# An RWKV block with a soft MoE behind it: three banks of g per block through DMA planes, the decayed state on ScalarE, a new order list

## The chip, the cores and the metric

The kernel runs on one core of one Trainium2 chip. The metric is the device time of one launch in microseconds. The engines are named as in the profile: PE (TensorE), with its weight loads shown apart as PEld, DVE (VectorE), ACT (ScalarE), POOL (GpSimd) and SP (SyncE, which here only issues DMAs). All inputs and outputs are float32.

## The reference

Three layers follow one another. The shapes: 4 batches, 8 heads, 768 steps, 48 values per head, so 3072 tokens of 384 values; 2048 hidden values; 8 experts of 4 slots each.

```python
# attention: a state per batch and head, decayed by w at each step
for t in range(S):
    cur = einsum('bhd,bhe->bhde', u * k[t], v[t])
    y[t] = einsum('bhd,bhde->bhe', r[t], state + cur)
    state = w[t][..., None] * state + einsum('bhd,bhe->bhde', k[t], v[t])
# hidden layer on x = y as [3072, 384]
h = x @ w_in;  g = h * cos(h);  x = g @ w_out
# soft mixture of experts
logits = x @ phi                        # [3072, 32]
d = softmax over tokens;  c = softmax over slots
slots = d.T @ x;  per expert: relu(slots @ w1) @ w2;  out = c @ slots_out
```

The kernel never forms `g @ w_out` for all tokens. It multiplies phi into w_out first, so that the logits come from g by a product with a 2048x32 matrix (`p_sb`), and it sums `d.T @ g` over the tokens (`E`) before w_out is applied.

## The kernel before

**Blocks and banks.** The 3072 tokens are 24 blocks j of 128 (6 per batch). Attention works on one block in two chunks c of 64 tokens: with scans over the decays (`scan`, `sp`), transposes of w, r and k, and matmuls A, U and y. The state goes from chunk to chunk: `e_z` (line 258) multiplies `st_state` by the decay over a chunk and gives z, 128x192; `e_rz` (267) has ACT copy z into the operand of y; `e_st` (271) adds the chunk's U to z and gives the next `st_state`. At the first chunk of a batch z is zeroed instead, so 44 of the 48 are products, all on DVE.

The hidden layer of a block t is four banks q of 128 tokens x 512 hidden values. `b_h` (423) makes one bank in PSUM with nine matmuls; `turns` (ACT), `rest` (DVE), `cos` (ACT) and `mul` (DVE) turn it into g, and the PSUM bank is free after `mul`. Two PSUM buffers hold h, up to bank number `ATT`; from there on h takes a buffer of attention's pool.

**Two ways to turn a bank.** The logits need g with hidden values on the partitions. In the first way four PE transposes (`gT`, `b_t`, line 466) write a PSUM bank and ACT (some of the last banks DVE) copies it out (`gc`, 474). In the second, through planes, `gz` (481) splits the 32-bit words of g into two planes of 16-bit halves, on ACT for every third bank and on GpSimd for the others (`GSPLIT`), `gd` (488) stores both planes in DRAM and `gx` (492) brings them back with a transposing DMA. Both DMAs are issued from SP's queue. Then four small matmuls (`l`, 496) add the bank to the logits. Banks 12 to 75, blocks 3 to 18, go through planes; the others use PE. There are four buffers for split planes and four for transposed banks. Banks that PE transposes use one PSUM buffer before bank `ATT`, and the pool of h from there on.

**Order.** `HEAD` (917) is a list of step names. The steps are issued in this order, and each engine, SP's queue too, runs its own instructions in the order of the list; an instruction waits at the head of its engine until what it needs is there. SP's queue carries the loads of w, r, k and v (`lw`, `lr`, `lk`, `lv`: one DMA per block each; `lz`: four), the planes' DMAs, and the expert weights.

**The end.** After every two blocks the logits go through an online softmax (`sum` to `es`), in which `E` adds `d.T @ g`. At `att` attention's memory is given up and SP is handed the first six of 16 expert weights, of 1536 KB each; each load waits until the tiles that lay in its place are free. Four more replace the parts of w_in, and the rest follow. The code behind the list (752 to 913) makes slots, experts (`hidden`, `expert_out`) and outputs.

Of the kernel before, what the change touches and what calls it, by code (L numbers as in the profile page):

```python
# [921 lines left out]
d2a.i.4 ksn.1 lv.1 d2a.i.5 wf.2 raw.i.6 lk.2 d2b.i.4 lz.1 lr.2 abs.i.5 A.1 y.0 mask.1 q.o.0 xh.0 whi.4 lw.3 xm.0 d2b.i.5 xc.0 wn.4.1 rz.1.0 wc.4.1
d2a.o.0 U.1 lz.2 scan.2 st.1.0 abs.o.0 d2b.o.0 raw.o.1 sr.2 wn.4.0 whi.5 z.1.1 q.i.7 q.i.6 lr.3 h.0.0 abs.i.7 oT.0 d2a.i.7 ru.2 lv.2 wc.4.0 oc.0
st.1.1 wn.5.0 kT.2 turns.0.0 wc.5.0 rz.1.1 d2a.i.6 sp.2 wn.5.1 wc.5.1 abs.i.6 wT.3 z.2.0 wf.3 ks.2 kN.2 rest.0.0 raw.o.2 lw.4 d2b.i.7 ksn.2 y.1 oT.1
d2b.i.6 scan.3 xh.1 rT.2 oc.1 xm.1 cos.0.0 whi.6 xc.1 abs.o.1 h.0.1 lk.4 mul.0.0 L.2 q.o.1 gT.0.0 U.2 bo.2 st.2.0 wn.6.1 sr.3 whi.7 d2a.o.1 wc.6.1
# [8 lines left out]
mul.1.2 rz.4.1 oT.15 h.2.0 gc.1.1 z.6.0 d2a.o.6 oc.15 kT.5 oc.14 sp.5 lw.8 wf.6 d2b.o.6 close gT.1.0 lw.7 ks.5 l.0.2 turns.2.0 bo.5 rT.5 gc.1.0 lr.7
oT.13 oc.13 z.5.0 oT.12 ru.6 rest.2.0 cos.2.0 gT.1.2 l.1.0 l.1.1 y.4 oc.12 L.5 xh.4 bs.5 gc.1.2 D.5 om.3 rT.6 xm.4 kN.5 turns.2.1 mul.2.0 scan.6 sr.6
xc.4 pc.3 bo.6 gT.1.3 lk.7 h.2.2 sp.6 pT.3 ksn.5 gc.1.3 rest.2.1 gT.2.0 bs.6 L.6 l.1.2 ps.3 l.1.3 l.0.3 U.5 turns.2.2 rest.2.2 A.5 cos.2.1 sum.0
rz.6.0 rz.5.0 lc.0 gc.2.0 lv.7 mul.2.1 st.5.0 h.2.3 mask.5 max.0 cos.2.2 kT.6 lz.6 mul.2.2 exp.0 z.5.1 wT.7 gT.2.1 h.3.0 turns.2.3 xt.0 ks.6 rest.2.3
# [4 lines left out]
mask.7 kT.8 gz.3.1 lk.9 rz.7.0 U.7 mul.4.1 bo.8 gz.4.1 gx.3.2 gd.3.1 turns.4.0 rest.4.0 gx.3.3 st.7.0 gx.3.0 bs.8 gx.3.1 h.4.2 wT.9 cos.4.0 D.8 l.2.1
lr.10 es.0 l.3.0 turns.4.2 l.2.2 l.2.3 wf.9 lk.10 mul.4.0 l.3.1 gz.4.0 z.7.1 ks.8 l.3.2 rest.4.2 l.3.3 gd.4.0 sum.1 A.8 lc.1 cos.4.2 scan.9 st.7.1
mask.8 kN.8 rz.7.1 max.1 h.5.0 mul.4.2 kT.9 ksn.8 exp.1 gx.4.0 xt.1 turns.5.0 sr.9 z.8.0 U.8 rest.5.0 cos.5.0 h.4.3 ks.9 ru.10 xr.1 st.8.0 xd.1 lw.11
gz.4.2 mul.5.0 wT.10 turns.4.3 dT.1 kN.9 rz.8.0 z.8.1 rest.4.3 st.8.1 dc.1 cos.4.3 lr.9 lz.8 ltok.1 gz.5.0 bo.10 sp.9 h.5.1 E.1.0 ksn.9 mul.4.3 lv.9
# [4 lines left out]
sp.11 bo.12 l.5.1 gx.5.2 turns.6.3 st.10.0 gx.5.3 D.10 A.10 rest.6.3 z.10.1 lv.11 l.4.3 rest.6.0 cos.6.3 z.12.0 l.5.2 st.10.1 cos.6.0 mul.6.3 rz.10.1  # L950
kT.11 ru.11 l.5.3 gz.6.3 sum.2 lz.9 gz.6.1 mul.6.0 ks.11 lz.10 es.1 h.6.2 gz.6.0 lc.2 mask.10 max.2 turns.6.2 gd.6.0 rest.6.2 kN.11 wT.12 bo.11 exp.2
xt.2 cos.6.2 rT.11 h.7.1 z.11.0 xr.2 mul.6.2 wf.12 xd.2 turns.7.1 rest.7.1 cos.7.1 gz.6.2 lr.13 y.9 dT.2 dc.2 L.11 lw.13 ltok.2 ksn.11 h.7.0 U.11
scan.12 E.2.0 lk.13 st.11.0 rz.11.0 y.10 mul.7.1 xh.9 turns.7.0 cmb.0.0 h.7.3 bs.11 gd.6.3 rest.7.0 xh.10 D.11 z.11.1 xl.9 gz.7.1 gd.6.1 lz.11 sr.12
# [104 lines left out]
```

## Time and profile before

| | us |
|---|---|
| three timed runs | 502.78, 502.20, 499.11 |
| their median | 502.2 |
| the profiled execution | 500.44 |
| its span, from the first to the last instruction | 498.7 |

| engine | busy us | share of the span | instructions |
|---|---|---|---|
| PE | 453.5 | 91% | 6261 |
| PEld | 340.1 | 68% | 6261 |
| DVE | 421.5 | 85% | 819 |
| ACT | 322.2 | 65% | 684 |
| POOL | 145.2 | 29% | 169 |

The mean granted clock of PE over the span is 0.993 of full speed. The chain that ended last, followed back from the last instruction, lies on PE for 56% of the span, on DVE for 14%, on DMA for 11%, on ACT for 6%, on SP's queue for 4% and on POOL for 2%; 5% is time in which the engine waited for nothing that is shown.

Busy time of PE is a union: matmuls overlap in the pipe, a single one lasts longer than the distance to the next, and the drain of the pipe before a wait counts as busy. In a group of instructions the first number after the bar is the sum of their durations, the second the mean of one; what follows the second bar is the idle time of the engine just before them, and what ended it.

### The profile page before, as it was taken

Reading aid. Unit: us, or ns where it says so; the run is one execution under the profiler, and the core shown is the slowest. Engines: PE = TensorE matmul, PEld = TensorE weight load, DVE = VectorE, ACT = ScalarE, POOL = GpSimd, SP = SyncE. Lnnn points to the kernel's source line nnn. Section 1 sums busy time; section 2 is a strip of 40 time slices with the busy share of each in tenths; the row PEclk is TensorE's granted clock in tenths of the full one; section 3 lists DMA queues with packets and bytes.
Section 4 is the critical chain, followed back from the end, with each engine's and each line's share of the span. In section 5 each row is a group of like instructions: output and inputs, shape, how many; then the busy total and the mean of one; then the engine's idle time right before and its main releaser. Section 6 shows DMA issues by size and latency. Waiting matters only on the chain.

```text
span 498.7 us, 15329 instructions
## 1 busy us (share of the span) xinstructions
PE 453.5 (91%) x6261; PEld 340.1 (68%) x6261; DVE 421.5 (85%) x819; ACT 322.2 (65%) x684; POOL 145.2 (29%) x169
## 2 busy tenths in 40 slices
PE   1678999999999899997999998998999999998993
PEld 1456788887777577765867666676777787865573
DVE  3999999999989999997999998997999976765242
ACT  5699998877575576664565864675656764664242
POOL 2422233323323705423334344223612100002110
PEclk9999999999999999998999999999999999999998
DMA  9999978346989969999498899988995579789938
GB/s 229 298 278 219 178 209 147 66 77 138 153 142 203 194 144 202 216 148 225 113 191 209 152 216 198 192 188 166 147 215 132 113 282 411 283 343 356 348 104 278
DMA packets 221188, 101.01 MB, mean 203 GB/s; under 512 B 195776, under 2 KB 201152, under 8 KB 221120
## 3 DMA queue, kind: packets, MB, share of 16 engines
q1 hardware_dynamic: 221120, 100.05, 86.7%
q8 instruction: 49, 0.80, 0.7%
q14 instruction: 19, 0.16, 0.1%
HBM read 61.75 MB, written 21.50 MB: 167 GB/s over the span
## 4 chain that ended last, share of the span: by engine, by line
PE 56%; DVE 14%; DMA 11%; ACT 6%; issue 5%; SPq 4%; POOL 2%; ACTq 0%; POOLq 0%; DVEq 0%
PE h L437 9%; PE h L439 8%; PE h L438 8%; DMA gx<-gs 7%; PE l L503 3%; PE E L599 3%; PE gT L471 3%; DMA rn<-in_r_dram 2%; PE y L283 2%; PE hps L790 2%; PE so L827 2%; PE A L204 2%; DVE pt L166 2%; PE U L255 2%; DVE g L456 2%
## 5 line engine op out<-in xcount | busy, mean ns | idle before, releaser
L437 PE MATMUL h<-wu,x 128*128 128x512 f32 (+1 forms) x288 | 122.3, 425 | 1.6 <-DVE g L464 1.6
L439 PE MATMUL h<-wu,x 128*128 128x512 f32 (+1 forms) x288 | 113.6, 395 | 0.0
L438 PE MATMUL h<-wu,x 128*128 128x512 f32 (+1 forms) x288 | 113.1, 393 | 0.0
L460 ACT ACTIVATE g<-g,half_pi 128x512 f32<-128x512 f32 (+1 forms) x97 | 69.4, 719 | 37.8 <-DVE g L456 37.0
L452 ACT ACTIVATE g<-h 128x512 int32<-128x512 f32 (+1 forms) x96 | 57.0, 596 | 53.3 <-PE h L439 43.2
L485 POOL COPY zg<-g 128x1024 uint16<-128x1024 uint16 x42 | 46.6, 1112 | 117.3 <-DVE g L464 72.1
L456 DVE SCALAR_TENSOR_TENSOR g<-g,h 128x512 f32<-128x512 int32 (+1 forms) x96 | 64.8, 677 | 11.3 <-ACT g L452 10.5
L464 DVE TENSOR_TENSOR g<-g,h 128x512 f32<-128x512 f32 (+1 forms) x96 | 64.3, 675 | 4.6 <-ACT g L460 3.9
L437 PEld LDWEIGHTS h<-wu,x 128*128 128x128 f32 x288 | 54.5, 189 | 17.3 <-DVE g L464 3.4
L439 PEld LDWEIGHTS h<-wu,x 128*128 128x128 f32 x288 | 54.3, 189 | 12.4
L438 PEld LDWEIGHTS h<-wu,x 128*128 128x128 f32 x288 | 54.5, 189 | 8.7
L218 POOL TENSOR_SCALAR_AFFINE_SELECT lt<-bo 64x512 f32<-64x512 f32 x48 | 35.5, 740 | 82.8 <-ACT bo L246 68.0
L171 POOL TENSOR_TENSOR ru<-rn,u_b 128x384 f32<-128x384 f32 x24 | 26.2, 1091 | 49.7 <-DMA rn<-in_r_dram 27.1
L230 DVE COPY_PREDICATED lt<-cs,A 64x256 f32<-64x256 uint32 x72 | 32.3, 448 | 2.8 <-PE A L204 1.4
L269 ACT COPY rzs<-z 64x192 f32<-64x192 f32 x96 | 33.3, 347 | 2.0 <-PE y L283 1.2
L187 DVE TENSOR_TENSOR lt<-rT,pt 64x512 f32<-64x512 f32 x48 | 32.8, 683 | 1.0 <-PE rT L143 0.4
L166 DVE TENSOR_TENSOR_SCAN pt<-wf,ini_f 128x520 f32<-128x520 f32 x24 | 32.8, 1367 | 0.1
L158 DVE TENSOR_TENSOR_SCAN qt<-wf,one_b 128x520 f32<-128x520 f32 x24 | 30.1, 1253 | 0.6 <-ACT wf L153 0.5
L503 PE MATMUL l<-gx,p_sb 128*32 128x128 f32 x512 | 23.4, 280 | 7.6 <-DMA gx<-gs 7.4
L172 POOL TENSOR_TENSOR ru<-ru,kn 128x384 f32<-128x384 f32 x24 | 27.9, 1163 | 4.5 <-DMA kn<-in_k_dram 2.7
L283 PEld LDWEIGHTS y<-lt,rzs 128*32 128x32 f32 x1536 | 23.9, 110 | 6.6 <-issue 5.3
L599 PE MATMUL E<-g,dt 128*32 128x512 f32 (+1 forms) x208 | 25.2, 567 | 2.4 <-ACT dt L580 1.6
(175 smaller groups left out, 807.3 us busy)
## 6 DMA issues: line engine op xcount, KB each, us to landing
we<-in_moe_w_dram SPq DMA_DIRECT2D x16, 1536.0 KB, 9.1
gs<-zg SPq DMA_DIRECT2D x64, 256.0 KB, 3.3
rawo<-in_moe_w_out_dram SPq DMA_DIRECT2D x8, 768.0 KB, 4.5
wn<-in_w_dram SPq DMA_DIRECT2D x24, 192.0 KB, 4.5
rn<-in_r_dram SPq DMA_DIRECT2D x24, 192.0 KB, 4.5
kn<-in_k_dram SPq DMA_DIRECT2D x24, 192.0 KB, 4.6
vn<-in_v_dram SPq DMA_DIRECT2D x24, 192.0 KB, 4.0
rzs<-in_v_dram SPq DMA_DIRECT2D x96, 48.0 KB, 3.0
```

Of the source, the lines that this page charges most:

```text
L166: nc.vector.tensor_tensor_scan(pt, wf[:, 0:NS * SEG], ini_f, 0.0, ALU.mult, ALU.add)
L218: nc.gpsimd.affine_select(out=lt[j % 2][h, a], in_=bo_t[j][h, a].unsqueeze(2).to_broadcast([64, NS, C]), pattern=[[0, NS], [-1, C]], compa ...
L437: nc.tensor.matmul(half[:, f], lhsT=xh[:, c, :], rhs=wh, start=(c == 0), stop=False)
L438: nc.tensor.matmul(half[:, f], lhsT=xl[:, c, :], rhs=wh, start=False, stop=False)
L439: nc.tensor.matmul(half[:, f], lhsT=xh[:, c, :], rhs=wl, start=False, stop=(c == KD - 1))
L452: nc.scalar.activation(gt.bitcast(I32), hp, AF.Copy, bias=0.25, scale=1.0 / TWO_PI)
L456: nc.vector.scalar_tensor_tensor(out=gt, in0=gt.bitcast(I32), scalar=-TWO_PI, in1=hp, op0=ALU.mult, op1=ALU.add)
L460: nc.scalar.activation(gt, gt, AF.Sin, bias=half_pi[:, 0:1])
L464: nc.vector.tensor_tensor(out=gt, in0=gt, in1=hp, op=ALU.mult)
L485: copy(zg, g_t[t, q].bitcast(U16).rearrange("p (f i) -> p i f", i=2))
L503: nc.tensor.matmul(lps_t[g][32 * m:32 * m + 32, o:o + TB], lhsT=p_sb[:, 4 * q + m, :], rhs=gt[:, m * 128:(m + 1) * 128], start=first, stop ...
L599: nc.tensor.matmul(ps[32 * q:32 * q + 32, cols], lhsT=dt_[:, tt, :], rhs=g_t[2 * g + tt, q][:, cols], start=(tt == 0), stop=(tt == 1))
```

## The change

- Banks with q = 3 no longer go through planes, but banks 0 to 2 of block 19 do: 51 banks (blocks 3 to 19, three each) instead of 64. The sixteen banks q = 3 of blocks 3 to 18 are transposed by PE, the three of block 19 no longer.
- All planes are split by GpSimd (`GSPLIT = "p"`).
- From block `JZ` = 5 on, z is made by ACT, as four activations with a scale per partition, one for each pair of heads. `JZP` = 24 lies beyond the last block, so GpSimd makes none.
- `ATT` goes from 77 to 81: four more banks of h stay in the pool of two buffers.
- `GMUL` could put `mul` on GpSimd; its list of q is empty, so no bank is.
- The order list is a new one from its first entries on. After `y.23`, the last step on PE that attention has, 13 banks of h follow in the list before and 8 in the new one; after `att`, 6 in both. In the new list, the step that comes next on ACT after the z of block 5 and later is a `cos` or `turns` in 23 of 35 cases.

```diff
@@ -43,10 +43,12 @@
     NTW = 6
     NLATE = 3
     JA = 6
+    JZ, JZP = 5, 24
     NSPLIT = 4
-    ATT = 77
-    GX = range(12, 76)
-    GSPLIT = "app"
+    ATT = 81
+    NGS = 51
+    GMUL = (12, 80, [])
+    GSPLIT = "p"
     NZG = 4
     NGX = 4
     ORDERED = {mybir.EngineType.PE, mybir.EngineType.DVE, mybir.EngineType.Activation, mybir.EngineType.Pool, mybir.EngineType.SP}
@@ -67,7 +69,7 @@
     ps_l = ps_stack.enter_context(tc.tile_pool(name="ps_l", bufs=1, space=PSUM))
     ps_m = ps_stack.enter_context(tc.tile_pool(name="ps_m", bufs=1, space=PSUM))
     ps_a = ps_stack.enter_context(tc.tile_pool(name="ps_a", bufs=3, space=PSUM))
-    gs_p = ctx.enter_context(tc.tile_pool(name="gs", bufs=len(GX), space=bass.MemoryType.DRAM))
+    gs_p = ctx.enter_context(tc.tile_pool(name="gs", bufs=NGS, space=bass.MemoryType.DRAM))
     a_stack = ctx.enter_context(ExitStack())
     nat = a_stack.enter_context(tc.tile_pool(name="nat", bufs=1))
     aw = a_stack.enter_context(tc.tile_pool(name="aw", bufs=2))
@@ -261,7 +263,11 @@
             nc.vector.memset(z, 0.0)
         else:
             pc = segs(q_t[j][0], 1, 1).rearrange("p (s c) j -> p s c j", c=2)
-            nc.vector.tensor_tensor(out=z, in0=st_state, in1=pc[:, :, c, :].to_broadcast([128, HP, D]), op=ALU.mult)
+            if j < JZ:
+                (nc.vector if j < JZP else nc.gpsimd).tensor_tensor(out=z, in0=st_state, in1=pc[:, :, c, :].to_broadcast([128, HP, D]), op=ALU.mult)
+            else:
+                for p in range(HP):
+                    nc.scalar.activation(z[:, p], st_state[:, p], AF.Copy, scale=pc[:, p, c])
         z_t[j, c] = z
 
     def e_rz(j, c):
@@ -461,7 +467,8 @@
 
     def b_mul(t, q, hf=None):
         gt, hp = bank(t, q, hf)
-        nc.vector.tensor_tensor(out=gt, in0=gt, in1=hp, op=ALU.mult)
+        pool = GMUL[0] <= NBK * t + q < GMUL[1] and q in GMUL[2]
+        (nc.gpsimd if pool else nc.vector).tensor_tensor(out=gt, in0=gt, in1=hp, op=ALU.mult)
 
     def b_t(t, q):
         gt = g_t[t, q]
@@ -915,99 +922,98 @@
 
 
 HEAD = """
...
-cs neg raw.i.1 q.i.1 raw.i.0 abs.i.1 d2a.i.1 q.i.0 lw.0 lw.1 wT.0 lr.0 abs.i.0 raw.i.3 d2b.i.1 lk.0 misc d2a.i.0 whi.1 d2b.i.0 wT.1 wf.0 scan.0 sr.0
...
-gx.8.1 mul.9.1 ksn.13 lw.15 rest.9.0 gd.8.2 sp.13 bs.13 h.9.3 cos.9.0 lw.16 xh.11 mul.9.0 rT.13 D.13 turns.9.3 gz.9.1 z.13.0 h.9.2 wf.14 xl.11
...
-gT.20.0 rest.20.3 turns.20.1 xl.22 gx.18.2 cos.20.3 y.23 cmb.2.2 l.18.2 l.19.1 l.19.2 l.19.3 mul.20.3 rest.20.1 l.18.3 cmb.2.3 xh.23 gT.20.3 cos.20.1
...
+raw.i.1 q.i.1 raw.i.0 d2a.i.1 abs.i.1 cs lw.0 q.i.0 z.0.0 lw.1 abs.i.0 lk.0 d2b.i.1 lr.0 d2a.i.0 d2b.i.0 wT.0 rz.0.0 misc wf.0 whi.0 neg wT.1 raw.i.3
...
+mul.9.2 wf.14 es.3 h.10.1 turns.10.0 rest.10.0 z.13.0 gz.9.2 ru.14 cos.10.0 gx.9.0 gT.9.3 gx.8.1 L.13 turns.10.1 mul.10.0 l.9.0 bs.13 rest.10.1 l.8.0
...
+cos.21.2 mul.21.2 gT.21.2 h.21.1 xh.22 es.9 gc.20.2 turns.21.0 xl.22 y.23 rest.21.0 l.20.2 cos.21.0 l.20.3 turns.21.1 mul.21.0 gc.21.2 gT.21.0 gc.21.0
...
```

## Rows read from the trace of the kernel before

**Rows 1.** Windows (stretch, length, busy us and count per engine, clock, DMA, GB/s)

```profile
95.00:395.00 300.00, 283.95 (x4073) 212.39 (x4067) 279.45 (x560) 192.99 (x419) 111.40 (x115) 0.99 0.89 169
395.00:453.00 58.00, 55.45 (x585) 41.62 (x586) 41.63 (x99) 35.16 (x78) 0.00 (x0) 1.00 0.86 318
```

**Rows 2.** Waits of PE, 95:345 (for whom: total us, times, longest)

```profile
PE l L503 <- DMA gx<-gs: 7.4, 8, 2.9
PE h L437 <- DVE g L464: 1.6, 3, 1.0
PE kT L143 <- DVE st_state L272: 1.3, 1, 1.3
...
PE A L204 <- DVE st_state L272: 0.8, 1, 0.8
```

**Rows 3.** Waits of PEld, 95 to 345 us

```profile
PEld l L503 <- DMA gx<-gs: 11.5, 13, 3.2
```

**Rows 4.** Timeline of PE, 229:240 (start, us, what, idle before it)

```profile
230.92 0.42 PE L503 MATMUL l<-gx,p_sb 128*32 128x128 f32 x8 [2.93 <-DMA gx<-gs]
```

**Rows 5.** Windows of the stretch behind that wait

```profile
231.00:235.00 4.00, 4.00 (x20) 2.99 (x21) 1.16 (x3) 0.21 (x1) 1.04 (x1) 0.65 1.04 276
```

**Rows 6.** Timeline of SP's queue, 222 to 232 us

```profile
223.34 1.51 SPq L490 DMA_DIRECT2D gs<-zg  x3
224.91 5.61 SPq L494 DMA_TRANSPOSE gx<-gs  x3
```

**Rows 7.** Issues of SP by line: ns min/median/max

```profile
L494 SPq DMA_TRANSPOSE gx<-gs x64: 1226/1292/3645, 124.3 to 395.5; - x64
...
L490 SPq DMA_DIRECT2D gs<-zg x64: 332/524/2352, 120.0 to 393.5; - x64
```

**Rows 8.** Chain of waits, 440 to 480 us (start, us, what)

```profile
443.28 0.44 PE gT L471 x4
...
473.81 5.36 PE so L827 x96
```

**Rows 9.** Groups by line, whole run (busy us, mean ns, idle before)

```profile
L485 POOL COPY zg<-g 128x1024 uint16<-128x1024 uint16 x42 | 46.6, 1112 | 117.3 <-DVE g L464 72.1 <-issue 40.5 <-ACT g L452 4.1
...
L269 ACT COPY rzs<-z 64x192 f32<-64x192 f32 x96 | 33.3, 347 | 2.0 <-PE y L283 1.2
...
L485 ACT COPY zg<-g 128x1024 uint16<-128x1024 uint16 x22 | 23.0, 1044 | 1.3 <-DMA gx<-gs 0.8
...
L477 ACT COPY gt<-gT 128x512 f32<-128x512 f32 x25 | 14.5, 585 | 5.1 <-PE gT L471 3.2 <-PE l L503 1.9
...
L246 ACT COPY bo<-bo 64x4 f32<-64x4 f32 x48 | 9.3, 193 | 1.8 <-DVE bo L241 0.7
...
L550 ACT ACTIVATE z<-dl,nb 128x65 f32<-128x65 f32 (+1 forms) x11 | 3.9, 351 | 0.5 <-DVE nb L529 0.2
```

**Rows 10.** Groups by line, DVE, 95 to 395 us

```profile
L264 DVE TENSOR_TENSOR z<-st_state,qt 128x192 f32<-128x192 f32 x34 | 16.5, 484 | 0.1
```

**Rows 11.** The decayed state's line over the run: ns min/median/max

```profile
L264 DVE TENSOR_TENSOR z<-st_state,qt x44: 296/351/1461, 21.9 to 390.5; 128x192 f32<-128x192 f32 x44
```

**Rows 12.** Timeline of all engines, 218 to 220 us

```profile
218.90 1.03 POOL L485 COPY zg<-g 128x1024 uint16<-128x1024 uint16 x1
218.99 1.16 DVE L264 TENSOR_TENSOR z<-st_state,qt 128x192 f32<-128x192 f32 x1
```

**Rows 13.** Windows of the end of the run

```profile
400.00:430.00 30.00, 30.00 (x307) 23.21 (x306) 21.19 (x50) 17.04 (x36) 0.00 (x0) 1.00 0.93 363
430.00:440.00 10.00, 9.89 (x58) 7.45 (x57) 7.33 (x20) 6.81 (x18) 0.00 (x0) 1.00 0.60 190
440.00:472.00 32.00, 29.08 (x432) 18.78 (x434) 15.60 (x41) 14.40 (x36) 4.76 (x6) 1.00 0.99 382
```

**Rows 14.** Timeline of PE, 402 to 404 us

```profile
402.51 1.10 PE L283 MATMUL y<-lt,rzs 128*32 128x64 f32 x64
```

**Rows 15.** The page's slices: GB/s in 40 slices

```profile
GB/s 229 298 278 219 178 209 147 66 77 138 153 142 203 194 144 202 216 148 225 113 191 209 152 216 198 192 188 166 147 215 132 113 282 411 283 343 356 348 104 278
```

More of the change, by code (lines that the diff above doesn't have):

```diff
@@ L922 @@
[L922 to L925, printed above, removed]
@@ L934 @@
[L934 to L937, printed above, removed]
@@ L942 @@
[L942 to L945, printed above, removed]
@@ L950 @@
[L950 to L953, printed above, removed]
@@ new lines @@
+oT.14 gc.1.1 d2b.o.6 close rz.4.1 xc.3 sp.5 turns.2.0 lz.5 oT.15 oc.14 oc.15 gT.1.0 l.0.2 wf.6 rest.2.0 rT.5 ru.5 oT.12 gc.1.0 oc.12 oT.13 oc.13
+gT.1.2 cos.2.0 bo.5 l.1.0 ru.6 z.5.0 y.4 gc.1.2 om.3 scan.6 L.5 mul.2.0 bs.5 pc.3 turns.2.1 lw.7 xh.4 l.1.1 kT.5 gT.1.3 D.5 sr.6 pT.3 ps.3 h.2.2 xm.4
+ks.5 rest.2.1 bo.6 cos.2.1 sp.6 kN.5 mul.2.1 gc.1.3 bs.6 rT.6 gT.2.0 turns.2.2 z.6.0 L.6 l.1.2 rest.2.2 l.1.3 l.0.3 ksn.5 sum.0 xc.4 lk.7 A.5 rz.5.0
+U.5 lc.0 mask.5 lv.6 cos.2.2 h.2.3 max.0 kT.6 exp.0 gc.2.0 D.6 mul.2.2 turns.2.3 lr.7 xt.0 st.5.0 ru.7 z.5.1 xr.0 h.3.0 wT.7 rest.2.3 ks.6 xd.0 gT.2.1
@@ new lines @@
+turns.6.0 ksn.10 sum.2 mul.6.3 U.10 lc.2 rest.6.0 scan.11 max.2 lv.11 gz.6.1 h.6.2 cos.6.0 mul.6.0 gT.6.3 D.10 exp.2 lz.9 xt.2 xr.2 ru.12 turns.6.2
+lz.10 rest.6.2 st.10.0 lr.11 cos.6.2 sr.11 xd.2 h.7.1 dT.2 A.10 mul.6.2 dc.2 ltok.2 turns.7.1 mask.10 h.7.0 z.10.1 kT.11 rz.9.1 st.10.1 gz.6.0
+rest.7.1 gz.6.2 cos.7.1 sp.11 z.11.0 mul.7.1 E.2.0 turns.7.0 E.2.1 gd.6.0 y.9 rT.11 gd.6.1 gc.6.3 ks.11 bo.12 rest.7.0 rz.10.1 ru.11 cos.7.0 gd.6.2
+h.7.3 L.11 gx.6.0 wT.12 mul.7.0 xh.9 gz.7.0 turns.7.3 kN.11 bo.11 rest.7.3 ksn.11 xl.9 cos.7.3 h.7.2 cmb.0.0 lv.12 mul.7.3 lw.13 wf.12 turns.7.2 bs.11
@@ new lines @@
+scan.14 gd.9.2 cos.10.1 U.13 st.13.0 sr.14 D.13 mul.10.1 h.10.2 A.13 gx.8.2 rz.13.0 bo.14 gz.10.0 gx.9.1 h.10.3 mask.13 wT.15 gc.9.3 kT.14 l.8.1
+gx.9.2 l.9.1 turns.10.2 z.13.1 rz.12.1 l.8.2 lr.15 l.9.2 sp.14 l.8.3 turns.10.3 st.13.1 rest.10.2 l.9.3 cos.10.2 y.12 rest.10.3 sum.4 lz.13 ks.14 lc.4
+lv.14 cos.10.3 ru.15 mul.10.2 rT.14 wf.15 gd.10.0 mul.10.3 max.4 xh.12 L.14 h.11.1 kN.14 rz.13.1 exp.4 xt.4 xr.4 h.11.0 gz.10.2 turns.11.1 xd.4
+gz.10.1 rest.11.1 ksn.14 z.14.0 cos.11.1 gx.10.0 xl.12 dT.4 lw.17 U.14 y.13 dc.4 ltok.4 mul.11.1 E.4.0 gd.10.2 st.14.0 rz.14.0 xh.13 h.11.3 scan.15
@@ new lines @@
+gx.11.0 z.15.1 st.15.1 rz.15.0 l.10.3 es.4 turns.12.1 l.11.0 rest.12.1 bo.17 wf.17 gx.11.1 A.15 h.12.3 scan.17 gx.11.2 l.11.1 rz.15.1 cos.12.1
+mul.12.1 mask.15 l.11.2 xh.14 gz.12.0 l.11.3 lw.19 z.16.0 turns.12.3 kT.16 xl.14 sum.5 ru.16 lc.5 gz.12.1 rest.12.3 h.13.0 max.5 exp.5 ks.16 xt.5
+lw.18 cos.12.3 gz.12.2 turns.13.0 wT.18 lz.15 sr.17 xr.5 mul.12.3 rT.16 kN.16 gd.12.0 xd.5 bo.16 ksn.16 dT.5 rest.13.0 lz.16 bs.16 dc.5 gd.12.2 h.13.1
+ltok.5 L.16 cos.13.0 E.5.0 mul.13.0 U.16 rz.16.0 lr.18 cmb.1.0 turns.13.1 lv.17 st.16.0 rest.13.1 h.13.2 D.16 z.16.1 gd.12.1 cos.13.1 sp.17 wf.18
@@ new lines @@
+gx.13.2 gx.13.0 cos.14.3 cmb.1.3 wf.19 mul.14.3 h.14.2 gd.14.0 gc.13.3 rT.18 scan.19 l.13.0 l.13.1 turns.14.2 xh.16 bs.18 l.13.2 gz.14.1 l.13.3
+rest.14.2 l.12.3 gT.14.3 lz.17 cos.14.2 sum.6 L.18 h.15.1 lc.6 mul.14.2 xl.16 max.6 kT.18 lv.19 turns.15.1 A.17 exp.6 rest.15.1 xt.6 ks.18 h.15.0
+gd.14.1 lr.20 xr.6 D.18 cos.15.1 z.18.0 gx.14.0 xd.6 kN.18 mask.17 dT.6 ksn.18 l.14.0 U.18 ltok.6 mul.15.1 lw.21 gx.14.1 st.18.0 dc.6 lk.20 ru.19
+sr.19 gz.14.2 rz.18.0 l.14.1 E.6.0 turns.15.0 wT.20 sp.19 h.15.2 rest.15.0 gz.15.1 kT.19 bo.19 z.18.1 st.18.1 gd.14.2 wf.20 E.6.1 cos.15.0 turns.15.2
@@ new lines @@
+mul.15.0 gz.15.0 rest.15.2 lz.18 A.18 gd.15.1 ks.19 gx.14.2 cos.15.2 mul.15.2 lk.21 h.15.3 mask.18 kN.19 bs.19 gc.14.3 rz.17.1 turns.15.3 ksn.19
+rest.15.3 h.16.1 cos.15.3 turns.16.1 lw.22 rT.19 y.17 scan.20 gz.15.2 mul.15.3 rest.16.1 z.19.0 D.19 xh.17 gd.15.0 gd.15.2 h.16.0 rz.18.1 gx.15.1
+cos.16.1 ru.20 L.19 xl.17 gx.15.0 mul.16.1 turns.16.0 rest.16.0 gx.15.2 gT.15.3 U.19 sr.20 st.19.0 cos.16.0 gc.15.3 h.16.3 sp.20 rz.19.0 z.19.1
+turns.16.3 es.6 wT.21 l.15.0 mul.16.0 lz.19 l.14.2 st.19.1 l.15.1 l.15.2 l.15.3 l.14.3 gz.16.0 gd.16.0 lw.23 rest.16.3 wf.21 scan.21 A.19 sum.7 kT.20
@@ new lines @@
+gc.22.3 cos.23.3.0 rest.23.3.1 cmb.2.5 E.10.0 mul.23.3.0 h.22.2 turns.23.0 rest.23.0 gT.22.0 cos.23.2 mul.23.2 cos.23.3.1 cos.23.0 turns.22.2
+mul.23.3.1 we.9 mul.23.0 gc.22.0 h.23.1 rest.22.2 gT.23.0 cos.22.2 turns.23.1 mul.22.2 l.22.0 l.22.1 gT.22.2 rest.23.1 gc.23.0 gT.23.2 l.23.0 gc.22.2
+cos.23.1 l.22.2 mul.23.1 l.22.3 gT.23.1 we.6 gc.23.2 gT.23.3 gc.23.3 we.7 gc.23.1 l.23.1 tab l.23.2 l.23.3 sum.11 lc.11 E.10.1 quart.11 max.11 exp.11
+late0 dT.11 ltok.11 dc.11 E.11.1 E.11.0 es.10 we.8 cmb.2.6 esl.11.1 esl.11.0 cmb.0.6
```

135 lines of the change are left out of this document (61 added, 74 removed).

## Prediction

> **What bounds the kernel now.** I first read busy time by stretch [rows 1]. From 95 to 395 us, where attention blocks and hidden banks run together, PE is busy 283.95 of 300 us and DVE 279.45; ACT has 107 us to spare, GpSimd 189. From 395 to 453 us PE is busy 55.45 of 58 and nothing competes with it. So what is to be won lies in the first stretch: 16 us in which PE has nothing to do. PE is the bound on average, but DVE at 93% is so close that every wait on it is likely to be felt.
>
> Next the waits of PE in that stretch [rows 2]. The largest is not DVE's: the logits matmuls stand 7.4 us, 8 times, for a plane that its transposing DMA has not delivered. Then come waits for DVE; the three largest, 1.6 for a product g, 1.3 and 0.8 for a new state, make 3.7. The weight loads wait longer for planes, 11.5 us [rows 3]: the 4.1 us between the two figures is time in which the matmul pipe drains and still counts as busy. One plane wait is 2.93 us long [rows 4], and behind it the granted clock is 0.65 on average over 4 us [rows 5], so part of that stretch went at the lower level, 1.2 of 2.4 GHz: at 0.65 about 35% of the 4 us, 1.4 us, was lost on top.
>
> Why the plane was late is seen on SP's queue [rows 6]: three stores of planes and three transposes fill it from 223.3 to 230.5, back to back. One transpose takes SP 1.29 us, one store 0.52, by their medians [rows 7]. SP is a third resource near its limit here.
>
> **The change, part by part.** *Planes.* Sixteen banks (the fourth of blocks 3 to 18) leave the planes, three (0 to 2 of block 19) enter; 64 planes become 51. On PE each bank that leaves costs four transposes, 0.44 us in the chain [rows 8]: +7.0 us before 395, -1.3 after, **+5.7 us**. PE is the bound there, so I charge it in full. SP loses 13 x (1.29 + 0.52) = 23.5 us of issuing, and the DMA engines 13 stores and 13 transposes. The plane waits with their clock loss are 7.4 + 1.4 = 8.8 us; between none and all of it goes. A fifth fewer planes on a queue that is full should take more than its share, and the loads of r, k and v behind them come sooner too: I take two thirds, **-6**. Of the drained 4.1, and as much again behind waits on DVE, **-3** (0 to -5).
>
> *The copies into planes.* ACT loses 22 x 1.044 = 23.0 us, GpSimd gets 9 more of 1.11, 10 us [rows 9]. GpSimd has the room; what waits is the plane behind it, and SP behind that, since each store is in SP's order: 0, with up to +3 if GpSimd's queue stands behind a load of r. Transposed banks are copied out of PSUM: sixteen more on ACT and two fewer, and DVE loses the one of bank 77: 14 x 0.585 = +8.2 us on ACT [rows 9]. All 45 such copies share one PSUM buffer up to bank 80; in the list a block's transposes come about once per block, so the buffer is free: 0, at most +1. The same bound holds for the four banks whose h stays longer in the two-buffer pool.
>
> *The decayed state.* Of 44 products, 35 leave DVE (38 from block 5 on, less the three that are zeroed). In the stretch one costs 484 ns [rows 10], 351 at the median and up to 1461 [rows 11]: the long ones stand beside a GpSimd copy, as at 218.99, where the product took 1.16 us while the copy that began at 218.90 ran [rows 12]. So 35 x 0.484 = 16.9 us of DVE go, stalls included; by the median 12.3. The Trainium skill (GPSIMD Engine Reference, Key points) says the same of instructions with two SBUF inputs, and its Perfetto Trace Analysis (Optimizing Scalar/DVE Operations) warns that moving work between GpSimd and VectorE might not help; the scans still have two SBUF inputs and meet nine more copies, which by that rule would leave the median's 12.3 rather than 16.9.
>
> DVE's idle time in the stretch rises from 20.5 to 37.4 us. Waits on an engine shrink roughly as its spare time grows: 20.5/37.4 = 0.55, so of the 3.7 us **-1.7** go (0 to -3.7).
>
> On ACT each product becomes four instructions of 128x48 with a scale per partition. The nearest rows are a 64x4 copy, 193 ns, a 64x192 copy, 348, and a 128x65 activation with an operand per partition, 351 [rows 9]. Between the copies 48 columns would be 229 ns; I take 290, halfway to 351, as the operand is there but the function is simpler: 1.16 us a product, 40.6 in all. The Trainium skill (ScalarE: Activation LUTs, Rules for kernel authors) says to multiply on VectorE rather than ScalarE, and budgets about 0.3 us plus 0.83 ns an element; an estimate by it is 1.36 us a product, 47.6 in all. Net, ACT gains 26 us on 107 spare, so the sum gets 0. It is not free of risk: ACT waits in order, and a product stands at the head of its queue until DVE has added the state before it; in the list 23 of the 35 have a turns or cos next behind them on ACT, and PE waits for those through DVE and the two h buffers. Cover gone, this is the second rival.
>
> *The list.* The order is new from its first entries on. The part that I can price is the end: after the last y, 13 hidden banks followed, now 8. From 402.51 [rows 14] to the last bank's transposes at 443.28 [rows 8] one bank takes 3.1 us, so attention ends some 15 us later against the end. SP sends the first six expert weights as attention's tiles come free, so they come later, and DMA has to make it up: against 411 GB/s, the highest slice of the page [rows 15], the time from 400 to 472 leaves 48 x 30 + 221 x 10 + 29 x 32 = 4.6 MB unused [rows 13], 11 us. 15 - 11 leaves 4 us, less than the last weights have in hand if they have landed by 472 and serve the end of the matmuls that run to 479 [rows 8]. I take 0 (up to +7). The first 95 us and the end hold the same work; 0 (-2 to +2).
>
> Sum: 5.7 - 6 - 3 - 1.7 = **-5.0 us**. The profiled execution took 500.4 us, its span 498.7; the three timed runs have the median 502.2. With the profiled one the middle of the four is 501.3, and I set the sum against that: **496.3 us**; that is 495.4 from the profiled execution and 497.2 from the median.
>
> **Rivals.** *DVE was the bound.* If PE's idle time was the shadow of a full DVE and SP, all of it goes. Then the stretch is PE's busy time, 284 + 7 = 291 us, 9 less, and 1.3 go after it: 490 us. For it: DVE at 93%, and attention is now spread over five more banks. Against: a third of PE's named waits are of other kinds.
>
> *ScalarE becomes the wait.* If one in three of the 23 x 1.16 us reaches PE, that is +8.9 (10.4 by the page's price), and with +5.7 and half of the relief, -5.5, the time is 501.3 + 9.1 = 510 us. It decides once ACT's queue has less than 1.16 us in hand before a turns. For it: the state's chain goes from DVE to ACT and back twice per block. Against: in the stretch ACT is busy 193 us, and would be some 220 of 300.
>
> *The waits move.* The relief is real but the order list sets who waits: planes come in time, something else is late, and PE has 5.7 us more work: 501 to 507, I say 504. For it: the rest of PE's waits are scattered over many lines.
>
> *Weights come late.* The forecast plus 6: 502 us.
>
> *It does not do what it says* only in two harmless parts: the list of banks whose product goes to GpSimd is empty, and the limit for GpSimd's decayed state is never reached.
>
> **How the numbers follow.** Forecast 0.40 (its own range 492 to 501), DVE 0.20, waits move 0.18, ScalarE 0.13, weights 0.09. The range of 8 in 10 is **486 to 507**: DVE's case with 4 us of room for a new list below, the waits that move above; most of ScalarE's case is left out. A per cent, which is about what this kernel's runs can tell, is 5 us: under 497.2 lie DVE's case and over half of the forecast, 0.45; over 507.2 most of ScalarE's and the edge of the moved waits, 0.18; between, 0.37.
>
> **What would show it.** From block 5 on, DVE's decayed state gone and its busy share in the stretch below 90%; four short ACT instructions per product of 0.23 to 0.35 us; plane waits of PE under 3 us in all and no stretch at a low clock behind one; PE busy 5 to 6 us more. Wrong would be: PE waiting for turns or the new state more than 5 us, or for expert weights.

## The result: 485.0 us after, 500.7 before, and the profile after

The changed kernel took **485.02 us** (median of four runs, 484.38 to 485.73); the kernel before, run on the same chip, 500.65 (four runs, 497.31 to 502.78). The ratio is 0.969, with the interval 0.963 to 0.976. The forecast was 496.3 with the range 486 to 507: the sign was right, the forecast gain was a third of what came, and the measured time lies just below the range. The profiled execution took 484.42 us with a span of 482.6, which is 16.1 us less than before.

Windows of the kernel after (stretch, length, busy us and count of PE, PEld, DVE, ACT, POOL, granted clock, DMA share, GB/s):

```profile
0.00:95.00 95.00, 79.86 (x1092) 61.65 (x1093) 84.07 (x122) 82.05 (x161) 27.03 (x45) 1.00 0.87 209
95.00:395.00 300.00, 296.61 (x4192) 229.55 (x4194) 277.89 (x560) 218.83 (x566) 117.06 (x123) 1.00 0.82 159
395.00:482.60 87.60, 75.41 (x1038) 54.60 (x1027) 42.78 (x103) 38.96 (x91) 6.68 (x10) 0.98 0.84 306
```

The first and last of these stretches in the kernel before, which [rows 1] does not have:

```profile
0.00:95.00 95.00, 76.74 (x1003) 59.51 (x1007) 84.47 (x123) 79.61 (x154) 27.09 (x45) 1.00 0.91 209
395.00:498.70 103.70, 92.83 (x1199) 68.18 (x1196) 57.56 (x138) 49.56 (x114) 6.69 (x10) 0.98 0.81 292
```

These rows and [rows 1] account for all 16.1 us. PE's idle time falls from 18.3 to 15.1 us in the first 95 us (-3.1), from 16.05 to 3.39 from 95 to 395 (-12.7), and rises from 10.9 to 12.2 behind that (+1.3). PE's busy time is 1.6 less (453.5 to 451.9), although it has 52 more transposes. DVE is as busy from 95 to 395 us as before, 277.89 against 279.45: the state's products are gone, but more banks fit into the same 300 us.

Waits of PE after, 95 to 345 us (for whom: total us, times, longest), to be read against [rows 2]:

```profile
PE dT L580 <- ACT ksn L236: 0.9, 1, 0.9
PE E L606 <- ACT dt L587: 0.7, 1, 0.7
PE E L606 <- DVE ltok L593: 0.7, 1, 0.7
PE U L257 <- DVE lt L232: 0.3, 1, 0.3
```

No wait for a plane is left, and none for a product g or a new state. The page's chain after (section 4) says the same in one line; before, PE had 56% of it, DMA 11% and SP's queue 4%:

```profile
PE 75%; DVE 11%; ACT 9%; issue 2%; DMA 2%; SPq 0%; ACTq 0%; DVEq 0%
```

Groups by line after (busy us, mean ns, idle before), for the moved work; they answer to [rows 9] and [rows 10]:

```profile
L478 PE MATMUL gT<-cs,g 128*128 128x128 f32 x180 | 26.9, 276 | 0.1
L510 PE MATMUL l<-gx,p_sb 128*32 128x128 f32 x408 | 16.5, 277 | 0.0
L492 POOL COPY zg<-g 128x1024 uint16<-128x1024 uint16 x51 | 56.2, 1109 | 107.7 <-DVE g L471 74.6 <-issue 19.3 <-PE h L445 6.5
L270 ACT ACTIVATE z<-st_state,qt 128x48 f32<-128x48 f32 x140 | 35.2, 324 | 2.9 <-DVE st_state L278 2.5
```

The number behind the bar is a union of the instructions' times, not their sum, as the section on the profile before has it: 140 x 324 ns would be 45.4 us. So the 140 activations are 35 products at 35.2/35 = 1.01 us. Four in a row on the timeline of ACT after (start, us, what):

```profile
218.41 1.00 ACT L270 ACTIVATE z<-st_state,qt 128x48 f32<-128x48 f32 x4
```

And the chain of the kernel after at its end (start, us, what), beside [rows 8]:

```profile
425.95 0.44 PE gT L478 x4
...
457.46 5.36 PE so L834 x96
```

From these transposes to these matmuls it is 31.51 us; before it was 473.81 - 443.28 = 30.53. So the end gives back 1.0 us of what was won ahead of it.

### The profile page after: what moved, and what is told of

Its sections match the earlier page's. It is cut to its first block, busy times and chain, and to the rows that moved or that the text cites. A ratio compares the mean times of both kernels' runs of the same rounds, so it can differ in the third digit from the quotient of the medians.

```text
span 482.6 us, 15486 instructions
## 1 busy us (share of the span) xinstructions
PE 451.9 (94%) x6313; PEld 345.8 (72%) x6313; DVE 404.7 (84%) x783; ACT 339.8 (70%) x816; POOL 150.8 (31%) x178
## 4 chain that ended last, share of the span: by engine, by line
PE 75%; DVE 11%; ACT 9%; issue 2%; DMA 2%; SPq 0%; ACTq 0%; DVEq 0%
PE h L443 13%; PE h L445 12%; PE h L444 12%; PE E L606 4%; PE y L289 4%; PE gT L478 4%; PE l L510 4%; PE A L206 3%; PE hps L797 2%; PE so L834 2%; PE wT L145 2%; PE U L257 2%; PE rT L145 2%; PE kT L145 2%; PE kN L213 2%
## 5 line engine op out<-in xcount | busy, mean ns | idle before, releaser
L492 POOL COPY zg<-g 128x1024 uint16<-128x1024 uint16 x51 | 56.2, 1109 | 107.7 <-DVE g L471 74.6
L466 ACT ACTIVATE g<-g,half_pi 128x512 f32<-128x512 f32 x97 | 69.4, 718 | 23.4 <-DVE g L462 22.5
L458 ACT ACTIVATE g<-h 128x512 int32<-128x512 f32 x96 | 57.2, 596 | 40.5 <-PE h L445 32.3
L462 DVE SCALAR_TENSOR_TENSOR g<-g,h 128x512 f32<-128x512 int32 x96 | 64.9, 677 | 8.0 <-ACT g L458 6.6
L471 DVE TENSOR_TENSOR g<-g,h 128x512 f32<-128x512 f32 x96 | 64.6, 676 | 7.8 <-ACT g L466 6.6
L443 PEld LDWEIGHTS h<-wu,x 128*128 128x128 f32 x288 | 54.2, 188 | 15.8 <-DVE g L471 2.5
L173 POOL TENSOR_TENSOR ru<-rn,u_b 128x384 f32<-128x384 f32 x24 | 25.5, 1061 | 44.3 <-DVE bo L243 12.9
L270 ACT ACTIVATE z<-st_state,qt 128x48 f32<-128x48 f32 x140 | 35.2, 324 | 2.9 <-DVE st_state L278 2.5
L232 DVE COPY_PREDICATED lt<-cs,A 64x256 f32<-64x256 uint32 x72 | 32.2, 447 | 2.0 <-PE A L206 0.5
L160 DVE TENSOR_TENSOR_SCAN qt<-wf,one_b 128x520 f32<-128x520 f32 x24 | 31.3, 1305 | 1.1 <-ACT wf L155 1.1
L168 DVE TENSOR_TENSOR_SCAN pt<-wf,ini_f 128x520 f32<-128x520 f32 x24 | 30.2, 1257 | 0.1
L174 POOL TENSOR_TENSOR ru<-ru,kn 128x384 f32<-128x384 f32 x24 | 25.7, 1071 | 9.2 <-DMA kn<-in_k_dram 7.6
```

The costliest lines, as they stand in the source:

```text
L270: nc.scalar.activation(z[:, p], st_state[:, p], AF.Copy, scale=pc[:, p, c])
L443: nc.tensor.matmul(half[:, f], lhsT=xh[:, c, :], rhs=wh, start=(c == 0), stop=False)
L458: nc.scalar.activation(gt.bitcast(I32), hp, AF.Copy, bias=0.25, scale=1.0 / TWO_PI)
L462: nc.vector.scalar_tensor_tensor(out=gt, in0=gt.bitcast(I32), scalar=-TWO_PI, in1=hp, op0=ALU.mult, op1=ALU.add)
L466: nc.scalar.activation(gt, gt, AF.Sin, bias=half_pi[:, 0:1])
L471: (nc.gpsimd if pool else nc.vector).tensor_tensor(out=gt, in0=gt, in1=hp, op=ALU.mult)
```

## The experiments

"Old list" and "new list" are the order lists of the two kernels. "The parts" are the other edits: the fourth bank on PE, all planes from GpSimd, the decayed state (z) on ScalarE. Each kernel was timed beside the kernel before on the same chip; ratios are to that one. Differences between two experiments are of their medians. Most pairs come from different chips, on which the kernel before had medians of 500.65 to 502.76, so a difference of 2 us or less says little. `ATT` = 81 and the planes of block 19 go with the new list in all that follows; no run separates them from it.

### Parts without the list, list without the parts

The theory at this point was that the list and the parts work only together; the rival, that one of the two carries the gain alone. The old list with the parts replaces `gz`, `gd`, `gx` of each fourth bank by `gT` and `gc` in the places of `gd` and `gx` and keeps 48 planes. The new list without the parts puts `gz`, `gd` and `gx` of these banks at 18, 43 and 75% of the way from their `mul` to their `l`; these places were chosen, so the size of what follows holds for them alone.

`old_all`, the old list with all parts:

```diff
+    JZ, JZP = 5, 24
-    GSPLIT = "app"
+    GSPLIT = "p"
+ 16x: gz.t.3 gd.t.3 gx.t.3 -> gT.t.3 gc.t.3
```

> The list of before, with the other parts of the change put into it: bank 3 of blocks 3 to 18 transposed on PE (its transposes take the place of the plane's store in the list, the copy the place of the transposing DMA; one logits step near block 18 moves by a few places), all planes split by GpSimd, z on ACT from block 5 on. 48 planes. Theory A (SP's queue and DVE were relieved, and that shortens the run): at most 490 us, plane waits of PE under 2 us. Theory B (the new order list does it): 496 to 505 us, since PE has 7 us more work and the waits are set by the old order.

`new_none`, the new list without them:

```diff
-    JZ, JZP = 5, 24
-    NGS = 51
-    GSPLIT = "p"
+    JZ, JZP = 24, 24
+    NGS = 68
+    GSPLIT = "app"
+ 16x: gT.t.3 gc.t.3 -> gz.t.3 gd.t.3 gx.t.3
```

> The new list with the old parts: bank 3 of blocks 3 to 18 through planes again (split, store and transposing DMA put between the bank's product and its logits step at 18, 43 and 75 per cent of the way), 67 planes, every third split on ACT, z on DVE throughout. Theory A: 495 us or more, since DVE has its 16 us and SP its 16 planes back. Theory B: 490 us or less, PE having 7 us less work than in the changed kernel.

Measured: `old_all` 505.51 us (1.0069, 1.0036 to 1.0102), half a us above the 496 to 505 of its second theory, `new_none` 544.17 (1.084, 1.077 to 1.091). Neither half gains. Window of `old_all`, and its waits of DVE in it:

```profile
95.00:395.00 300.00, 286.81 (x4080) 216.56 (x4073) 267.76 (x520) 207.10 (x545) 118.26 (x120) 1.00 0.70 141
```

```profile
DVE g L462 <- ACT g L458: 7.6, 14, 1.2
DVE st_state L278 <- ACT z L270: 6.0, 7, 1.2
DVE g L471 <- ACT g L466: 5.9, 8, 1.3
```

The same waits in the changed kernel:

```profile
DVE g L462 <- ACT g L458: 4.4, 8, 1.2
DVE ltok L593 <- ACT dt L587: 2.9, 5, 1.1
DVE t L564 <- ACT z L557: 2.3, 6, 0.5
DVE g L471 <- ACT g L466: 1.5, 6, 0.5
```

With the parts in the old list the plane waits do go, but PE is still idle for 13 us in the stretch, and DVE waits 19.5 us for ScalarE's turns, cosines and z, against 5.9 us for turns and cosines and none for z in the changed kernel. DVE has more idle time than before, 32.2 us against 20.5, and yet PE's waits for a product g and a new state do not shrink; the largest in `old_all`, 95 to 395 us, beside 1.6 and 0.8 in [rows 2]:

```profile
PE h L443 <- DVE g L471: 2.2, 4, 1.0
PE A L206 <- DVE st_state L278: 1.3, 3, 0.6
```

That is the rival "the waits move", which had 504. In the new list without the parts, PE waits for planes, by its group over the run:

```profile
L510 PE MATMUL l<-gx,p_sb 128*32 128x128 f32 x536 | 25.4, 308 | 37.4 <-DMA gx<-gs 37.4
```

### One part at a time

Three of these need no edit of a list, so they isolate their part without a choice of mine: `new_z` (z back on DVE), `new_app` (every third bank's planes split by ScalarE again) and `old_z` (the old kernel with z on ScalarE alone).

```diff
# new_z: the changed kernel with
-    JZ, JZP = 5, 24
+    JZ, JZP = 24, 24
# new_app: the changed kernel with
-    GSPLIT = "p"
+    GSPLIT = "app"
# old_z: the kernel before with
+    JZ, JZP = 5, 24
# old_planes: old_all with
-    JZ, JZP = 5, 24
+    JZ, JZP = 24, 24
# new_planes: new_none with
-    JZ, JZP = 24, 24
+    JZ, JZP = 5, 24
# new_planes_p: new_planes with
-    GSPLIT = "app"
+    GSPLIT = "p"
```

> The changed kernel with z back on DVE (35 products of 0.35 to 0.48 us, 12 to 17 us of DVE). Theory A: 489 us or more, since DVE is over 92 per cent busy beside attention and each of its microseconds is felt. Theory B: at most 487 us; the list has slack for it.

> The changed kernel with every third plane split on ACT again (17 of 51), nothing else. If the copies on ACT matter little: 485 to 488 us. If the new list has no room on ACT for a 1.04 us copy at those places: 495 us or more, with SP waiting for ACT's copies 20 us or more, as it did 38 us in the run with 67 planes.

> The kernel before with one thing changed: z made by ACT from block 5 on, list and planes as they were. Theory A' (DVE's time is felt in either list): 494 to 498 us, the 6 us that the same step is worth in the new list. Theory B' (the old order takes no advantage of spare time on DVE): 499 to 506 us, waits of DVE for z on ACT taking the place of the product.

> The kernel before with bank 3 of blocks 3 to 18 transposed on PE and all planes split by GpSimd, z left on DVE. Theory A': 495 us or less, since PE's plane waits of 7.4 us go. Theory B': 502 to 507 us, 7 us of PE work against the plane waits, and other waits where the planes' were.

> The changed kernel with bank 3 of blocks 3 to 18 through planes again (67 planes, every third split on ACT), z left on ACT. Theory A: 490 us or more, with plane waits of PE of 5 us or more and SP's queue full. Theory B: 480 to 487 us, since PE loses 7 us of transposes.

> The changed kernel with bank 3 of blocks 3 to 18 through planes (67), all split by GpSimd, z on ACT. If the 57 us of the run with 67 planes came from the copies on ACT: at most 500 us. If they came from the planes themselves (SP's queue, four buffers for planes): 525 us or more, with plane waits of PE of 30 us or more.

| kernel | us | ratio to the kernel before |
|---|---|---|
| new_z | 491.21 | 0.979 (0.974 to 0.985) |
| new_app | 495.00 | 0.986 (0.981 to 0.992) |
| old_z | 505.20 | 1.0049 (1.0014 to 1.0083) |
| old_planes | 499.99 | 0.9951 (0.9914 to 0.9988) |
| new_planes | 542.65 | 1.080 (1.072 to 1.087) |
| new_planes_p | 527.80 | 1.049 (1.043 to 1.056) |

In the new list z on ScalarE is worth 491.2 - 485.0 = 6.2 us; in the old one it costs, by 2.5 us against the kernel before and by 505.5 - 500.0 = 5.5 beside the other parts. The same edit has a different sign in the two orders. In `new_planes` it moves nothing that can be told from noise (544.2 to 542.7). `old_planes`, the old list with the other two parts, came between its two theories: it gains 0.5%, and its interval lies below 1. The fourth bank through planes, at the places chosen, costs the new list 42.8 us even with all splits on GpSimd (527.8 against 485.0), and PE stands 29.4 us for planes there from 95 to 395 us. The split on GpSimd is worth 10.0 us in the new list with 51 planes; in the old list no run isolates it. Waits of SP's queue in `new_app`, 95 to 395 us:

```profile
SPq L497 <- ACT zg L492: 39.0, 10, 14.6
SPq L501 <- DMA gs<-zg: 18.5, 14, 4.4
SPq L497 <- POOL zg L492: 9.7, 8, 3.4
```

and, of the same stretch, the window, PE's wait for planes and DVE's for ScalarE's turns and cosines:

```profile
95.00:395.00 300.00, 288.42 (x4005) 221.30 (x4005) 271.33 (x534) 224.40 (x557) 98.61 (x105) 0.99 0.76 148
```

```profile
PE l L510 <- DMA gx<-gs: 3.2, 5, 0.8
```

```profile
DVE g L462 <- ACT g L458: 7.5, 12, 1.7
DVE g L471 <- ACT g L466: 3.8, 12, 0.7
```

The longest of SP's waits, 14.6 us, ends with the first store of the run, at 119.55 us. In the changed kernel the first store comes at 112.90, after that kernel's longest such wait, 6.3 us. So it stands at the start of the planes, not in their flow. In all, SP waits 48.7 us for splits, against 41.0 in the changed kernel. PE idles 8.2 us more than there from 95 to 395 us (11.58 against 3.39), and its waits for planes are 3.2 of that. DVE's two waits make 11.3 us, against 5.9. So late planes are named for a part only. The 17 copies are also 17.7 us of work on ScalarE; at the rate of `after_zz` below, 12.1 us for 31.6, an estimate of their cost by that alone is 6.8 us. No run separates the two.

### Pace or local order

One difference of the lists is the pace: in the new one one to five more banks of h stand ahead of a block's y from block 9 on (the "up to seven" below is a miscount). `old_pace` gives `old_all` the new pace, `new_pace` gives the changed kernel the old one. Each keeps the order within attention and within the banks and merges the two anew.

```diff
# old_pace, as an example: old_all's list with the steps of attention of block j >= 9
# moved back by as many banks of h as the new list has more of ahead of y.j
```

> The list before with both parts (bank 3 on PE, all planes from GpSimd, the decayed state on ScalarE), but with attention from block 9 on at the pace of the new list: up to seven banks of h more stand before a block's y, and eight instead of thirteen after the last y. The order within attention and within the banks stays the old list's. At the old pace this kernel took 505.5 us. Theory, the pace: attention spread over more banks is what lets PE fill its gaps; then at most 495 us, and PE's idle time from 95 to 395 us under 8. Rival, the local order (how far a producer stands ahead of its consumer): then 501 to 507 us, and the same waits for DVE and ScalarE stay.

> The changed kernel with attention at the pace of the list before (about as many banks of h before each block's y as there), the order within attention and within the banks as in the new list. The changed kernel took 485.0 us. The pace: at least 495 us. The local order: at most 489 us.

Measured: 580.07 us (1.154, 1.146 to 1.162) and 587.63 (1.170, 1.165 to 1.175). Window of `old_pace`:

```profile
95.00:395.00 300.00, 258.29 (x3426) 191.76 (x3424) 226.57 (x441) 174.81 (x456) 100.86 (x101) 0.95 0.61 123
```

`old_pace` lies 73 us above what either theory allowed; `new_pace` meets the letter of "at least 495", but a loss of 103 us is more than a change of pace explains while `old_all`, at that pace, takes 505.5. A likely reason, not shown, is that the merge lost what both lists have in common, the place of each attention step between the steps of a bank. These runs tell nothing on pace against local order; they show that the same steps in a coarser merge cost 75 to 103 us, with no kind of wait of PE above 7.3 us in that stretch. Which property of the new list makes the difference stays open.

### Who stands a delay, and who is the bound

The next runs add or take time on one engine in both orders, without touching the lists. `after_zz` and `old_zz` issue z's four activations twice; `old_z1` and `after_z1` make z with one activation.

```diff
# after_zz (changed kernel), old_zz (old_all)
-                for p in range(HP):
+                for p in list(range(HP)) * 2:
# old_z1 (old_all), after_z1 (changed kernel)
-                for p in range(HP):
-                    nc.scalar.activation(z[:, p], st_state[:, p], AF.Copy, scale=pc[:, p, c])
+                nc.scalar.activation(z, st_state, AF.Copy, scale=pc[:, 0, c])
```

> The changed kernel with the decayed state's four activations issued twice over, the second time onto the same values: some 35 us more on ScalarE from block 5 on, and about 1 us more in the state's chain, 35 times. Theory, slack: the new list has placed the producers of PE's operands far enough ahead that an engine with room may be late; then at most 4 us over 485.0. Rival, no slack (the new list only fits these very durations): 10 us or more over.

> The same doubling of the decayed state's activations in the list before with both parts, which took 505.5 us. Slack is what the old list lacks: 10 us or more over 505.5, with PE waiting for turns, the new state or products g. If both lists have the same slack: as much over 505.5 as the doubled kernel of the new list lies over 485.0, within 2 us.

> The list before with both parts, where the decayed state is one activation of 128x192 per product instead of four of 128x48 (all heads get the scale of the first pair: that part of the result is left out). That takes some 0.7 us from ScalarE and from the state's chain, 35 times. The kernel with four took 505.5 us. Theory, the order: what the old list lacks is not time on an engine, so even a nearly free decayed state leaves it at 496 us or more. Rival, ScalarE's load: then under 492 us, near the changed kernel.

> The changed kernel with the same cheaper decayed state (one activation of 128x192 with the scale of the first pair of heads). It took 485.0 us with four. Doubling the four cost 12 us; if the cost is linear, 0.7 us less on 35 products gives 6 to 8 us: 477 to 479. If PE is the bound, with 3.4 us idle left between 95 and 395 us, it can give at most that: 482 to 485.

The other four load DVE and PE: the reductions of bo twice, and the transposes of the fourth banks twice.

```diff
# after_dd (changed kernel), before_dd (kernel before)
-        nc.vector.tensor_reduce(out=own, ...)
+        for _ in range(2):
+            nc.vector.tensor_reduce(out=own, ...)
# after_gg (changed kernel), old_gg (old_all)
-        for m in range(4):
+        for m in list(range(4)) * (2 if q == 3 and 3 <= t <= 18 else 1):
```

> The changed kernel with the sum of r u k (24 reductions of 0.54 us on VectorE) made twice: 12.9 us more on VectorE, spread over the run. If VectorE is the bound in the joint stretch: 10 us or more over 485.0. If its idle 7% still takes it up, because its work lies where it isn't waited for: 1 to 5 us.

> The kernel before with the same reductions made twice, 13 us more on VectorE. If VectorE was the bound before the change: 10 us or more. If its order was, any shift of VectorE shows too, and more than in the changed kernel: as a multiple of it, 2 or more (the doubled decayed state cost 28 us in the old list, 12 in the new). Same slack in both: within 3 us of what it costs the changed kernel.

> The changed kernel with the four PE transposes of the sixteen added banks (fourth bank of blocks 3 to 18) issued twice onto the same PSUM bank: 16 x 0.44 = 7.0 us more on PE. If PE is the bound in the joint stretch, and a transpose is worth its distance in the chain: 6 to 8 us over 485.0. If PE's idle time takes it up: under 3.

> The same doubling in the list before with both parts, at 505.5 us, where PE was idle 13 of 300 us from 95 to 395. If PE's idle time there belongs to waits that stand anyway: 6 to 8 us more, as in the new list. If the idle time takes some of it up: 0 to 4. If each shift costs more than itself in that list, as with the doubled decayed state: over 10.

| kernel | us | ratio (interval) | base | moved | work added, busy us |
|---|---|---|---|---|---|
| after_zz | 497.13 | 0.991 (0.988 to 0.995) | 485.02 | +12.1 | ACT +31.6 |
| old_zz | 533.59 | 1.062 (1.057 to 1.067) | 505.51 | +28.1 | ACT +31.6 |
| after_z1 | 487.29 | 0.971 (0.966 to 0.977) | 485.02 | +2.3 | ACT -19.4 |
| old_z1 | 496.87 | 0.992 (0.989 to 0.994) | 505.51 | -8.6 | ACT -19.4 |
| after_dd | 492.45 | 0.981 (0.975 to 0.987) | 485.02 | +7.4 | DVE +13.3 |
| before_dd | 506.68 | 1.0105 (1.005 to 1.016) | 501.3 | +5.4 | DVE +13.2 |
| after_gg | 491.88 | 0.979 (0.973 to 0.985) | 485.02 | +6.9 | PE +7.0 |
| old_gg | 509.32 | 1.014 (1.008 to 1.019) | 505.51 | +3.8 | PE +6.9 |

The added work is the difference of the groups' busy time. For z it is 66.8 us (280 activations) or 15.8 us (35) against 35.2; for the other two, see the rows of `after_dd` (DVE, 12.9 us in the changed kernel) and of `after_gg`. The rows of `after_zz`, `after_dd` and `after_gg`:

```profile
L270 ACT ACTIVATE z<-st_state,qt 128x48 f32<-128x48 f32 x280 | 66.8, 322 | 2.8 <-DVE st_state L278 2.6
```

```profile
L244 DVE TENSOR_REDUCE bo<-ru 128x8 f32<-128x384 f32 x48 | 26.2, 546 | 0.8
```

```profile
L478 PE MATMUL gT<-cs,g 128*128 128x128 f32 x244 | 33.9, 275 | 0.0
```

On **PE** the new list charges the added work in full by the medians, 6.9 of 7.0 us (4.8 by the ratios to the kernel before); the old list takes up nearly half in its idle time. On **ScalarE** the new list gains nothing when 19.4 us are taken away, while the old list gains 8.6; 31.6 us more cost the old list 28.1 and the new one 12.1. Both edits change the chain from state to state too, by about as much for each product, so load on ScalarE and length of that chain are not told apart. "At most 4" for `after_zz` was wrong: the new list has slack, but not that much. On **DVE** both pay, 0.56 us for each us added in the changed kernel (0.43 by the ratios) and 0.41 in the kernel before, which has none of the parts. So the old order, which stands delays on ScalarE worse, does not stand them worse on DVE, and neither is charged in full; the expectations of `after_dd`, over 10 or under 5, both missed. `after_z1` missed both of its own, 477 to 479 and 482 to 485, and is 2.3 us above 485.0 (0.9 by the ratios), so no gain and no clear loss. `old_z1` bears out its theory, 496 us or more, by 0.9 us. Waits of DVE, 95 to 395 us, in `old_zz`:

```profile
DVE g L462 <- ACT g L458: 15.2, 15, 2.1
DVE g L471 <- ACT g L466: 12.1, 12, 2.2
DVE st_state L278 <- ACT z L270: 10.7, 7, 3.1
```

and in `after_zz`:

```profile
DVE g L471 <- ACT g L466: 7.3, 17, 1.0
DVE g L462 <- ACT g L458: 6.6, 9, 2.1
...
DVE st_state L278 <- ACT z L270: 4.1, 8, 1.0
```

In these rows DVE waits 38.0 us for ScalarE in the old list and 18.0 in the new one; before the doubling it was 19.5 and 5.9. The same added activations thus add 18.5 us of waits in the old list and 12.1 in the new one. So the new list has more slack between ScalarE and DVE; that this alone makes the difference of the two lists is not shown.

## Why the prediction was wrong, step by step

**The step that failed** is the pricing of relief by shares of the old list's waits, with 0 for the list and for the split: "I take two thirds, -6", "of the 3.7 us -1.7 go", "0 (-2 to +2)". In numbers: the sum took 5.1 + 1.7 = 6.8 us of PE's idle time away, and 14.5 went, of which 12.7 lie between 95 and 395 us. Part of the idle time of that stretch was in no named row: 16.05 us idle, and of the four rows of [rows 2] 11.1. The share for DVE's waits assumed that they shrink as DVE's idle time grows, from 20.5 to 37.4 us. It grew to 22.1 only, and the waits behind the 3.7 us went all the same; in `old_all` it grew to 32.2, and they did not shrink; in `new_z`, with the new list and 15.4 us of DVE's idle time, they are 0.5 us for a new state and 0.3 for a product g. No run shows the rule of the sum, and these three speak against it: as far as they show, those waits went with the new order, not with DVE's time. The plane waits went with the parts, in `old_all` too.

**Transposes on PE, +5.7: right**, as far as `after_gg` shows: 6.9 us by the medians for 7.0 us of the same transposes.

**Plane waits, -6: too small.** All 7.4 us went, and the clock of the stretch is 1.00 in place of 0.99.

**Drains, -3: too small.** PE's busy time is 1.6 less with 5.7 charged, so drains and the lower clock gave 7.3 together; the sum had 3 and 0.9 for them. How the 7.3 divide between the two no run separates. The sign "PE busy 5 to 6 us more" did not come for this reason.

**GpSimd's split, 0: wrong for the new list**, where it is worth 10.0 us (`new_app`). I counted ScalarE's spare time and asked only what could be lost. What is lost with splits on ScalarE is in part PE's waits for late planes, 3.2 us, and perhaps in larger part the copies' own load on ScalarE; the two are not separated.

**The decayed state.** The price was near: 1.01 us a product against 1.16. The Trainium skill (ScalarE: Activation LUTs, What ACT_TABLE_LOAD costs) gives 186 ns plus 0.833 ns an element, 93 more for an operand per partition, and 93 of overlap between neighbours; an estimate by it is 319 ns for one and 1.00 us for four. The trace agrees, with 321 ns at the median and 1.01. What it is worth was not a matter of price: -6.2 us in the new list, +2.5 in the old. The Trainium skill's rule (ScalarE: Activation LUTs, Rules for kernel authors) to multiply on VectorE rather than ScalarE goes by the price for each element. The trace has the lower price on VectorE too, with 351 ns a product at the median [rows 11] against 1.01 us; for the time of the kernel the rule came out in the old list and not in the new one. Of the five products of over 1 us on DVE in the kernel before, two ran beside a copy into planes and three beside GpSimd's products `ru`, so "the long ones stand beside a GpSimd copy" was too narrow.

**"DVE below 90%": wrong.** It is 92.6%, because the stretch now holds more work: 560 instructions of DVE as before, though 34 products are gone.

**The list at the end, 0 (up to +7): right.** The weights cost 1.0 us at most, by the rows of the chain. The first 95 us, which I had at 0 too, gave 3.1.

**The rivals.** "DVE was the bound" came nearest in time, 490, since most of PE's idle time in the stretch went, as it said; its cause is not borne out: 13.2 us more on DVE cost the kernel before 5.4, and DVE is as busy in the stretch after as before. So it is in part luck that the time came near. "The waits move" came true, at its own number, where the old list has the parts. "ScalarE becomes the wait" came true there too, with 5.5 us, and not in the new list, where a cheaper z wins nothing. (The list has a turns or cos next behind z in 22 of the 35 cases, not 23.)

Shown, then: neither all three parts nor the list gains alone in the forms tried (two of the parts gain 0.5% in the old list), together they bring PE to 99% from 95 to 395 us, and there PE is the bound. The one-part prices in the new list, 6.2 and 10.0, are not to be added: each is measured with the others in place. Not shown: which trait of the list it is.

## What to carry to other kernels

When a change comes with a new order of all queues, the waits of the old order are no price list: the price of an edit may change its sign with the order, so forecast from the idle time of the bound engine, with "all of it" as a case of its own and more weight than the named waits give it. A copy that feeds a queue of DMAs is worth trying on the engine with the shorter queue, even if the other has time to spare: here that gave 10.0 us in the final order, though why was not fully separated. To find who is the bound, double one small known cost on each engine in turn: where the time moves by all of it, that is the bound.
